# Attention with a gated FFN on one core: the loads of head 0 in order of need on one queue, its second block's query halves shifted by VectorE copies, later projections emitted sooner

## The chip, the cores and the metric

The kernel runs on one core of a Trainium2 chip. The metric is the device time of one execution in microseconds (us). A trace shows one run.

Names of engines: PE is TensorE (matmul), DVE VectorE, ACT ScalarE, POOL GpSimd, SP the engine that here only issues DMAs (the page lists no busy time for it). The granted clock is the share of TensorE's full pace that the trace records; "half clock" is 0.5. "L483" is a line of the kernel. The change shifts lines a little: L483 and L484 of before are L488 and L489 after it, L420 is L425, L425 is L430, L512 is L517.

## The reference

```python
xn = layernorm(x)                                   # x: 2048 x 640
q  = (xn @ wq) -> 32 heads of 192                   # k_cache, v_cache: 32 x 2048 x 192
s  = concat_heads(softmax(q k^T / sqrt(192)) v) @ wo
g  = silu((silu(x@w1) * (x@w3)) @ w2)               # the FFN gets xn too: 640 -> 1536 -> 640
out = x + s * g
```

Both parts get the normalised x. There are 32 heads, 4 blocks of 512 queries (`qb`), and 8 pairs of 128-key tiles (`p`) in a block. The work is one stream of (head, block, pair).

## The kernel before

Nearly all of it is TensorE: per pair six matmuls of scores (K times q), an exponential on ACT, and 16 matmuls of values. At `p == 0` of a block, TensorE also projects the queries of the *next* head for that block (`project`). Head 0 has no head before it, so its own projections (`project0`) stand inside its own stream, and everything they need is prepared while it runs: layer norm of x block by block on DVE, transposition of the normalised x (`xn`) into `xnT`, a copy of `xnT` with the two halves of the partitions swapped (`xnS`, by DMA), and for every q tile the pieces `qC` with its halves moved to the other partitions. K of later heads comes transposed by DMA (`load_k`); K of head 0 comes plain (`kn`) and is transposed by TensorE (`turn_k0`), copied by ACT, and one of its five windows is shifted to the other half of the partitions (`shift_k0`).

```python
    def load_k0():                                         # [cut]
        nc.scalar.dma_start(out=kn, in_=A_k_cache[0, 0].rearrange("(p t) d -> p (t d)", p=P))
    def shift_k0(j0):                                      # [cut]
        nc.vector.tensor_copy(out=KW[0:64, 3, ks], in_=KW[64:P, 0, ks])
    def move_q(qAB, qC, half):
        nc.gpsimd.dma_start(out=qC[0:64, half, :], in_=qAB[half][64:P, :])
        if half == 0:
            nc.gpsimd.dma_start(out=qC[64:P, 0, :], in_=qAB[0][0:64, :])
    def project0(qb):                                      # [cut: 10 matmuls from xnT]
        cast_pair(qAB, ps)                                 # qA by DVE, qB by ACT
        move_q(qAB, qC, 0)
        move_q(qAB, qC, 1)

    def head_start():
        load_x(0, 0, 2)                                    # SP's queue
        load_k0()                                          # ACT's queue
        load_x(0, 2, 4)
        load_w0()                                          # POOL's queue: weights of heads 0 and 1
        load_x(1)
        load_v(0)
        load_w(1)
        for g in range(2, NQB):
            load_x(g)
        turn_over(40)                                      # filler matmuls
        # [cut: layer norm of x block 0]
        turn_k0(pk0, 0, range(4)); copy_k0(pk0, 0); turn_over(6)
        ln_turn(0, 0, nc.vector.tensor_copy); turn_over(6) # transposes of xn
        # [cut: the other halves]
        swap_halves(0)                                     # xnS, SP's queue
        copy_k0(pk1, NPAIR // 2); project_first(); scores(0); shift_first()
        shift_k0(0); shift_k0(NPAIR // 2); scores(1)       # [cut]

    for n, (h, qb, p) in enumerate(stream):
        if p == 0 and n > 0: project(h + 1, qb)            # [cut]
        if h == 0 and qb == 0 and p == 3: project(1, 0)
        if h == 0 and qb + 1 < NQB and p == (6 if qb == 0 else 4):
            project0(qb + 1)
        scores(n + 2)                                      # two pairs ahead
        values(n)
        # [cut] for head 0: layer norm of block qb + 2 at p = 2 to 6, its transposes by DMA on SP's
        # queue; at p == 4 of block 0 the last x transposes of block 1;
        # at (qb == 1, p == 0) load_k(1), load_v(1) on SP's queue
```

All of this is in program order, and the order counts: in the change x's transposes stand behind kn's in TensorE's list and started at 11.09 us, after kn had come; put ahead of them (d_x_first below) they started at 8.14.

## Time and profile before

| | |
|---|---|
| time | 1954.48 us (3 runs, 1954.23 to 1954.80) |
| profiled span | 1952.9 us |
| PE busy | 1933.8 us, 99% |
| PE pauses in the first 75 us | 13.8 us in all |
| granted PE clock | 1.0 from its first record at 8.1 us on, but for 6.8 us after 35.4 us, when it was 0.5, and the end |

The page of the kernel before, the line of the engines' busy times and the first line of the chain that ended last:

```profile
PE 1933.8 (99%) x27281; PEld 1390.5 (71%) x27289; DVE 652.7 (33%) x990; ACT 1179.6 (60%) x1276; POOL 285.9 (15%) x511
...
PE 98%; DMA 1%; issue 0%; DVE 0%; POOL 0%; SPq 0%; DVEq 0%; POOLq 0%
```

So TensorE sets the time from end to end, and a change can only gain by taking pauses (or slow clock) out of TensorE's stream. These are the pauses of 1.5 us and more; all lie before 75 us. The columns are who waited, for whom, total us, how often, the longest (the three for qC are 3.04 us in block 1, 1.47 in block 2 and 0.45 in block 3):

```profile
PE st L484 <- DMA qC<-qA: 5.0, 3, 3.0
PE pk L564 <- POOL ident_bf masks.py:199: 2.8, 1, 2.8
PE st L483 <- DVE qA L425: 1.8, 1, 1.8
PE ps L420 <- DMA xnS<-xnT: 1.6, 1, 1.6
PE pst L352 <- DVE xn L344: 1.5, 1, 1.5
```

The largest lie together, at the first scores of block 1. TensorE's timeline there (start, duration, engine, line, operation, output<-inputs, and in brackets the idle time before it with what ended it):

```profile
34.78 0.39 PE L483 MATMUL st<-qA,KW 64*128 64x512 bf16 x1 [1.78 <-DVE qA L425]
38.21 0.58 PE L484 MATMUL st<-qC,KW 64*128 64x512 bf16 x1 [3.04 <-DMA qC<-qA]
```

TensorE projected block 1, needed the result at once, and stood until DVE had cast it and the DMAs had moved its halves. The second matmul took 0.58 in place of 0.38 us, at a granted clock of 0.50 (in each stretch of 1 us from 36 to 42 us). In the stretch from 35 to 40 us (last three columns: granted clock, DMA share, GB/s) it reads 0.54:

```profile
35.00:40.00 5.00, 1.96 (x12) 0.65 (x12) 0.74 (x2) 0.13 (x1) 1.59 (x3) 0.54 0.80 155
```

The loads of the start (last figure: median us from issue to landing):

```profile
kn<-in_A_k_cache_dram ACTq DMA_DIRECT2D x1, 768.0 KB, 5.4
vt<-in_A_v_cache_dram SPq DMA_DIRECT2D x1, 768.0 KB, 13.4
x_all<-in_A_x_dram SPq DMA_DIRECT2D x2, 320.0 KB, 5.8
W<-in_A_wq_dram POOLq DMA_DIRECT2D x2, 160.0 KB, 7.6
```

Last, what SP did for head 1 around that pause.

SP's timeline of issues, the load of K and V for head 1, then block 3's x transposes:

```profile
41.13 5.24 SPq L252 DMA_TRANSPOSE KW<-in_A_k_cache_dram  x1
46.42 2.89 SPq L253 DMA_TRANSPOSE KW<-in_A_k_cache_dram  x1
49.35 1.22 SPq L292 DMA_DIRECT2D vt<-in_A_v_cache_dram  x2
54.83 7.38 SPq L358 DMA_TRANSPOSE xnT<-xn  x4
```

### The profile page before, as it was taken

Reading aid. Unit: us, or ns where it says so; the run is one execution under the profiler, and the core shown is the slowest. Engines: PE = TensorE matmul, PEld = TensorE weight load, DVE = VectorE, ACT = ScalarE, POOL = GpSimd, SP = SyncE. Lnnn points to the kernel's source line nnn. Section 1 sums busy time; section 2 is a strip of 40 time slices with the busy share of each in tenths; the row PEclk is TensorE's granted clock in tenths of the full one; section 3 lists DMA queues with packets and bytes.
Section 4 is the critical chain, followed back from the end, with each engine's and each line's share of the span. In section 5 each row is a group of like instructions: output and inputs, shape, how many; then the busy total and the mean of one; then the engine's idle time right before and its main releaser. Section 6 shows DMA issues by size and latency. Waiting matters only on the chain.

```text
span 1952.9 us, 59687 instructions
## 1 busy us (share of the span) xinstructions
PE 1933.8 (99%) x27281; PEld 1390.5 (71%) x27289; DVE 652.7 (33%) x990; ACT 1179.6 (60%) x1276; POOL 285.9 (15%) x511
## 2 busy tenths in 40 slices
PE   7999999999999999999999999999999999999998
PEld 5677777777777777777777777777777777577776
DVE  6333333333333333333333333333333334521111
ACT  4667676767677767677777767776767677210000
POOL 3211111111111111111111111111111110000000
PEclk9999999999999999999999999999999999999999
DMA  8633242333343433353434332433323230837873
GB/s 189 126 61 89 56 96 60 96 68 94 64 100 68 100 68 100 67 157 68 100 67 101 68 98 67 100 68 75 88 58 96 58 82 2 242 77 139 155 151 60
DMA packets 394691, 179.57 MB, mean 92 GB/s; under 512 B 341648, under 2 KB 382864, under 8 KB 394432
## 3 DMA queue, kind: packets, MB, share of 16 engines
q1 hardware_dynamic: 372080, 125.98, 30.0%
q0 software_dynamic: 19760, 46.30, 9.9%
q8 instruction: 215, 3.52, 0.8%
q10 hardware_dynamic: 2592, 3.41, 0.6%
q14 instruction: 44, 0.36, 0.1%
HBM read 52.82 MB, written 27.79 MB: 41 GB/s over the span
## 4 chain that ended last, share of the span: by engine, by line
PE 98%; DMA 1%; issue 0%; DVE 0%; POOL 0%; SPq 0%; DVEq 0%; POOLq 0%
PE obank L512 35%; PE st L483 30%; PE ps L420 14%; PE ps_s L111 11%; PE st L484 3%; PE ps_f L718 3%; PE ps_gu L692 1%; DMA xnS<-xnT 0%; DMA qC<-qA 0%; DMA x_all<-in_A_x_dram 0%; PE ps L407 0%; DVE stats L316 0%; POOL qC L375 0%; DVE qA L425 0%; POOL rstd L325 0%
## 5 line engine op out<-in xcount | busy, mean ns | idle before, releaser
L486 ACT ACTIVATE pT<-st 128x1024 bf16<-128x1024 f32 x1024 | 1046.3, 1022 | 263.1 <-PE st L484 247.6
L512 PEld LDWEIGHTS <-pT 64*128 64x128 bf16 x16384 | 748.0, 94 | 209.0 <-issue 0.8
L512 PE MATMUL obank<-vt,pT 64*128 64x193 bf16 x16384 | 870.0, 244 | 0.0
L483 PE MATMUL st<-qC,KW 64*128 64x512 bf16 x2046 | 607.2, 377 | 0.3 <-DVE qC L393 0.3
L484 PE MATMUL st<-qC,KW 64*128 64x512 bf16 x1022 | 385.4, 377 | 5.0 <-DMA qC<-qA 5.0
L521 DVE COPY osum<-obank 128x772 f32<-128x772 f32 x128 | 123.1, 961 | 795.8 <-PE obank L512 795.8
L483 PE MATMUL st<-qA,KW 64*128 64x512 bf16 x1022 | 384.9, 377 | 2.0 <-DVE qA L425 1.8
L484 PE MATMUL st<-qB,KW 64*128 64x512 bf16 x1024 | 386.1, 377 | 0.0
L484 PE MATMUL st<-qA,KW 64*128 64x512 bf16 x1022 | 385.5, 377 | 0.0
L483 PEld LDWEIGHTS <-KW 64*128 64x128 bf16 x3068 | 278.2, 94 | 139.8 <-issue 7.9
L420 PE MATMUL ps<-xnT,W 64*128 64x512 bf16 x1280 | 299.4, 376 | 0.0
L420 PE MATMUL ps<-xnS,W 64*128 64x512 bf16 x1280 | 293.9, 377 | 1.6 <-DMA xnS<-xnT 1.6
L484 PEld LDWEIGHTS <-KW 64*128 64x128 bf16 x3068 | 279.0, 94 | 3.0 <-issue 2.1
L375 POOL DMA_DIRECT2D qC<-qA x127 | 66.7, 525 | 1298.4 <-DVE rl_all L528 1274.4
L420 PEld LDWEIGHTS <-W 64*128 64x128 bf16 x2560 | 141.7, 94 | 106.5 <-issue 1.9
L426 ACT CAST qB<-ps 128x512 bf16<-128x512 f32 x131 | 76.7, 585 | 230.1 <-PE ps L420 225.1
L111 PE MATMUL ps_s<-wo_sb,oT 128*128 128x384 bf16 (+3 forms) x1535 | 208.8, 300 | 0.1
L111 PEld LDWEIGHTS <-oT 128*128 128x128 bf16 x1536 | 148.1, 98 | 60.7
L522 DVE TENSOR_TENSOR osum<-osum,obank 128x772 f32<-128x772 f32 x128 | 122.7, 959 | 13.4
L529 DVE TENSOR_TENSOR ostage<-osum,rl_all 128x768 bf16<-128x768 f32 x128 | 122.6, 958 | 5.0 <-DMA o_scr<-ostage 0.7
L461 DVE SCALAR_TENSOR_TENSOR hT<-pt,qB 64x512 bf16<-64x512 bf16 x64 | 43.8, 684 | 199.1 <-ACT pt L460 199.1
L425 DVE CAST qA<-ps 128x512 bf16<-128x512 f32 x131 | 90.5, 691 | 29.5 <-PE ps L420 16.5
(79 smaller groups left out, 623.5 us busy)
## 6 DMA issues: line engine op xcount, KB each, us to landing
o_scr<-ostage SPq DMA_DIRECT2D x16, 1536.0 KB, 10.2
vt<-in_A_v_cache_dram SPq DMA_DIRECT2D x62, 384.0 KB, 5.5
qC<-qA POOLq DMA_DIRECT2D x254, 64.0 KB, 1.9
qC<-qB POOLq DMA_DIRECT2D x127, 64.0 KB, 2.3
wo_sb<-in_A_wo_dram POOLq DMA_DIRECT2D x1, 7680.0 KB, 36.3
W<-in_A_wq_dram POOLq DMA_DIRECT2D x32, 160.0 KB, 3.4
W<-in_B_w_dram POOLq DMA_DIRECT2D x32, 80.0 KB, 3.2
W<-in_A_wq_dram POOLq DMA_DIRECT2D x32, 80.0 KB, 2.9
```

What stands on the lines that cost most here:

```text
L111: nc.tensor.matmul(ps[:, 0:w], lhsT=oT[:, k, :], rhs=wo_sb[:, k, c0:c1], start=(k == 0), stop=(k == OC - 1))
L375: nc.gpsimd.dma_start(out=qC[0:64, half, :], in_=qAB[half][64:P, :])
L420: nc.tensor.matmul(ps[:, r * 512:(r + 1) * 512], lhsT=W[rows, j, :], rhs=xs[rows, j // 2, qs], start=(j == 0), stop=(j == 2 * DC - 1))
L425: a = nc.vector.tensor_copy(out=qAB[0][:], in_=ps[:, 0:512])
L426: b = nc.scalar.copy(out=qAB[1][:], in_=ps[:, 512:1024])
L483: nc.tensor.matmul(st2[:, 0:512], lhsT=ka, rhs=qa, start=r == 0 and nr == 3, stop=r == nr - 1)
L484: nc.tensor.matmul(st2[:, 512:1024], lhsT=kb, rhs=qb2, start=r == 0 and nr == 3, stop=r == nr - 1)
L486: nc.scalar.activation(out=pT2[:], in_=st2[:], func=ACT.Exp, scale=att_scale)
L512: nc.tensor.matmul(obanks[r][:, j * 256:j * 256 + DH + 1], lhsT=pT2[r * 64:(r + 1) * 64, t * 512 + j * P:t * 512 + (j + 1) * P], rhs=vt[r ...
L521: nc.vector.tensor_copy(out=osum[:], in_=ov[0])
L522: nc.vector.tensor_tensor(out=osum[:], in0=osum[:], in1=ov[1], op=ALU.add)
L529: nc.vector.tensor_tensor(out=ostage[:, qb * 4:qb * 4 + 4, hg * DH:(hg + 1) * DH], in0=osum[:, :, 0:DH], in1=rl.unsqueeze(2).to_broadcast( ...
```

## The change

Its intent: let x of block 0 come first and the rest of head 0's loads in the order in which they are needed, all on SP's queue; take the K shift off DVE; move block 1's query halves by DVE copies (0.29 us each) in place of DMAs; and emit the projections of blocks 1 to 3 one or two pairs sooner, so that casts and moves hide behind a pair.

```diff
 def load_k0():
-        nc.scalar.dma_start(out=kn, ...)
+        nc.sync.dma_start(out=kn, ...)
 def shift_k0(j0):
-        nc.vector.tensor_copy(out=KW[0:64, 3, ks], in_=KW[64:P, 0, ks])
+        nc.gpsimd.dma_start(out=KW[0:64, 3, ks], in_=KW[64:P, 0, ks])
 def project0(qb):
-        move_q(qAB, qC, 0)
-        move_q(qAB, qC, 1)
+        if qb == 1:
+            nc.vector.tensor_copy(out=qC[64:P, 0, :], in_=qAB[0][0:64, :])
+            nc.vector.tensor_copy(out=qC[0:64, 0, :], in_=qAB[0][64:P, :])
+            nc.vector.tensor_copy(out=qC[0:64, 1, :], in_=qAB[1][64:P, :])
+        else:
+            move_q(qAB, qC, 0)
+            move_q(qAB, qC, 1)
 def head_start():
         load_x(0, 0, 2)
+        load_x(0, 2, 4)
         load_k0()
-        load_x(0, 2, 4)
 [cut]
         load_w(1)
-        for g in range(2, NQB):
-            load_x(g)
 [cut]
         copy_k0(pk0, 0)
+        shift_k0(0)
 [cut]
         copy_k0(pk1, NPAIR // 2)
+        shift_k0(NPAIR // 2)
+        for g in range(2, NQB):
+            load_x(g)                       # now behind swap_halves(0) on SP's queue
         project_first()
         scores(0)
         shift_first()
-        shift_k0(0)
-        shift_k0(NPAIR // 2)
 main loop:
-        if h == 0 and qb + 1 < NQB and p == (6 if qb == 0 else 4):
+        if h == 0 and qb + 1 < NQB and p == (5 if qb == 0 else 2):
             project0(qb + 1)
```

More of the change, by code (lines that the diff above doesn't have):

```diff
@@ L261, in load_k0 @@
         kn = k0["kn"][:].rearrange("p t c -> p (t c)")[:, 0:NKT * DH]
-        nc.scalar.dma_start(out=kn, in_=A_k_cache[0, 0].rearrange("(p t) d -> p (t d)", p=P))
+        nc.sync.dma_start(out=kn, in_=A_k_cache[0, 0].rearrange("(p t) d -> p (t d)", p=P))
         k0["v"] = kn.rearrange("p (j c) -> p j c", c=2 * DH)
```

## The prediction

> **What bounds the kernel now.** TensorE: the page gives 1933.8 us busy of a 1952.9 us span (99%), and the chain of waits is 98% PE. All that can be won lies in the first 75 us; later the change touches nothing. TensorE's waits there (waits and timeline, 0 to 75 us): 2.75 us for the identity; 1.46 for the first normalised x (xn); 0.5+0.3+0.3 around the first scores; 1.56 for xnS, the swapped halves of xnT; 1.78 for the qA cast and 3.04 for the qC moves of block 1; 1.47 and 0.45 for the qC moves of blocks 2 and 3. The windows of 1 us show a granted clock of 0.50 from 36 to 42 us, so 38.21 to 42.86 holds work of 2.6 us at full pace: 2 us more. [...]
>
> **Costs and gains.**
> 1. kn moves from ACT's queue to behind x block 0 on SP's. Now the first x half lands at about 6.3 us, sharing 350 to 430 GB/s with kn. From cumulated bytes I estimate x half one at 4.3 us, kn at 7.1 (now 6.1). The warm-up ends at 7.0 anyhow, so kn's 16 transposes (1.58) and 6 fillers end near 9.1; there the x transposes start, not at 10.36. Gain 1.2 us (0.5 to 1.5).
> 2. x blocks 2 and 3 (1.3 MB) no longer precede the xnS swap, which took 9.6 us to land (later ones 3.6 to 5). The 1.56 us wait goes; about 0.2 remains for PSUM held by the qA cast. The K shift by DMA frees 0.5 us of DVE. Gain 1.4.
> 3. Block 1: project0 goes one pair earlier, and three DVE copies (0.29 each) replace DMAs of 1.9 to 2.8 us. The waits of 1.78 and 3.04 and the 2 us of clock go. New: project0 follows the transposes directly and waits about 0.9 us for DVE's xnT copy (0.82). Gain 6.
> 4. Blocks 2 and 3: project0 two pairs (2.6 us) earlier hides the moves: 1.47+0.45+0.2. But all is now 9 us earlier, and block 3's xnT transposes queue on SP behind the load of K for head 1 (issue 5.24+2.89 us). I expect project0 of block 3 to wait for xnT 0 to 2.6 us, and 0.3 us each for xnT of block 2 and for DVE freeing obank. Net 0.3.
>
> Sum: 1.2 + 1.4 + 6 + 0.3 = about 9 us, nearly all on the critical path, because TensorE hardly pauses afterwards. That is 0.5%.
>
> **Predicted time: 1945.5 us, 1942 to 1949 eight times in ten. Faster by over 2%: 0.01; within 2%: 0.98; slower: 0.01.**
>
> **What would show each step.** (1) First DVE statistics near 4.5 us, x transposes near 9. (2) No PE wait on xnS, landing in about 5 us. (3) No PE wait on qC in block 1, granted clock 1.0 from 30 to 45 us, a short wait on the xnT copy. (4) No wait on qC of blocks 2 and 3; possibly one on DMA xnT before block 3's projection. PE busy falls by about 2 us (clock); the time after 75 us is unchanged.
>
> **What would make it wrong.** kn landing after 8.5 us (gain 1 gone); the K shift, or V of head 0, late among the loads; x block 2 so late behind the swap that DVE holds the casts; the wait for block 3's xnT exceeding 3 us[...]. In the other direction, K's load issuing faster (3.0+2.4 us, as for head 2): 1944 or below.

1.2 + 1.4 + 6 + 0.3 is 8.9, its "about 9 us", and the 2 us of clock in the 6 is read from the trace of before (0.50 from 36 to 42 us).

## More of the kernel before

DVE's timeline, the norm of block 2's last two tiles:

```profile
34.94 0.80 DVE L344 TENSOR_SCALAR xn<-x_all,mv,rstd 128x640 bf16<-128x640 bf16 x2 [0.21 <-POOL rstd L325]
```

## The result

The changed kernel takes 1952.86 us (median of 4 runs, 1951.70 to 1953.43), the kernel before 1954.64 us (4 runs, 1954.23 to 1955.28). The ratio is 0.999, 95% interval 0.9973 to 1.0007. (A ratio here is the mean time of one kernel's fast runs over that of the other's of the same rounds, so not quite the ratio of the medians that are quoted.) Predicted was 1945.5 us, 1942 to 1949. It is the same within 2%, as predicted, but of the 9 us only 1.8 came, and the time lies outside the range.

The pauses of TensorE of 0.8 us and more in the first 75 us of the changed kernel, to be held against those of before:

```profile
PE ps L407 <- DMA xnT<-xn: 3.1, 1, 3.1
PE st L489 <- DMA qC<-qA: 3.0, 1, 3.0
PE pk L569 <- POOL ident_bf masks.py:199: 2.8, 1, 2.8
PE pk L272 <- DMA kn<-in_A_k_cache_dram: 2.6, 1, 2.6
PE st L488 <- DMA KW<-KW: 1.0, 1, 1.0
PE ps L407 <- DVE xnT L354: 0.9, 1, 0.9
PE obank L517 <- DVE osum L527: 0.8, 1, 0.8
```

The waits that the change aimed at are gone (qA, xnS, xn, and qC of block 1), and four others stand there, for kn, KW, xnT, and qC of block 2, which was 1.47 us before. All four are DMAs. Where they lie in TensorE's timeline:

```profile
9.85 1.07 PE L272 MATMUL pk<-ident_bf,kn 128*128 128x128 bf16 x16 [2.65 <-DMA kn<-in_A_k_cache_dram]
...
19.82 0.39 PE L488 MATMUL st<-qC,KW 64*128 64x512 bf16 x1 [0.97 <-DMA KW<-KW]
...
53.51 0.37 PE L489 MATMUL st<-qC,KW 64*128 64x512 bf16 x1 [2.97 <-DMA qC<-qA]
...
64.22 2.32 PE L407 MATMUL ps<-xnT,W 128*128 128x512 bf16 x9 [3.13 <-DMA xnT<-xn]
```

The loads of the start, now:

```profile
kn<-in_A_k_cache_dram SPq DMA_DIRECT2D x1, 768.0 KB, 8.1
vt<-in_A_v_cache_dram SPq DMA_DIRECT2D x1, 768.0 KB, 16.9
x_all<-in_A_x_dram SPq DMA_DIRECT2D x2, 320.0 KB, 3.2
...
W<-in_A_wq_dram POOLq DMA_DIRECT2D x2, 160.0 KB, 8.8
```

x of block 0 came 2.6 us sooner (3.2 against 5.8 us from issue), but kn took 8.1 where it had taken 5.4, V 16.9 where it had taken 13.4, and the weights 8.8 for 7.6. DVE's timeline of the changed kernel, block 2's last norms:

```profile
37.76 0.80 DVE L344 TENSOR_SCALAR xn<-x_all,mv,rstd 128x640 bf16<-128x640 bf16 x2 [0.81 <-POOL rstd L325]
```

SP's issues in the changed kernel, head 1's loads and block 3's transposes:

```profile
43.45 5.59 SPq L252 DMA_TRANSPOSE KW<-in_A_k_cache_dram  x1
49.08 4.28 SPq L253 DMA_TRANSPOSE KW<-in_A_k_cache_dram  x1
53.41 1.21 SPq L292 DMA_DIRECT2D vt<-in_A_v_cache_dram  x2
54.66 6.16 SPq L358 DMA_TRANSPOSE xnT<-xn  x4
```

The load of K for head 1 starts 2.3 us *later* than before, although TensorE is 6 us further: SP's list has block 2's x transposes in front of it, they wait for the norms, and DVE does the norms 2.8 us later. Between two norms DVE now waits 0.71 us for block 1's projection, does its cast and three copies (till 34.2 us), and then waits 0.85 us for ACT; before, it went straight on with the next work, and the cast came later.

### The ledger

The start of the same piece of work in both traces says where the time went. `best3` is the best kernel found, told below.

| TensorE starts, us | before | after | sooner by | best3 |
|---|---|---|---|---|
| first scores of head 0 | 15.66 | 16.30 | -0.64 | 14.66 |
| first projection of head 1 (in block 0) | 21.76 | 23.56 | -1.80 | 20.76 |
| scores that follow it | 25.66 | 25.72 | -0.06 | 22.92 |
| projection of head 1 in block 1 | 42.86 | 36.49 | +6.37 | 33.53 |
| the same in block 2 | 59.61 | 55.95 | +3.66 | 49.48 |
| the same in block 3 | 75.83 | 74.38 | +1.45 | 65.78 |
| end of the profiled span | 1952.9 | 1951.6 | +1.3 | 1942.8 |

Differences of neighbouring rows: the start lost 0.64, the K shift 1.16, the swap gained 1.74, block 1 gained 6.43, block 2 lost 2.71, block 3 lost 2.21. The sum is 1.45, and after 76 us nothing changes. Block 1 gave 6.43 of the 9 us that were promised. Of what had been gained at 36 us, 4.92 was given back within 40 us.

The first two rows are of one profile, and others share that start. d_kload_late, d_q2_dve, d_both and u_p4 (below) are the same program through block 0; in their traces the wait for kn (2.3 to 3.5 us) was followed by half clock (0.50 from 11 to 12 us in the first three; in u_p4 kn's 16 transposes took 1.86 us in place of 1.07), the first scores started at 17.20 to 18.79, and there was no wait for KW: from the first scores to head 1's first projection they took 6.10 us, as before the change. So the loss of 0.64 is the mildest of five, and the 1.16 of the K shift appears in this profile alone, where TensorE came to the shifted K soonest. By the first projection of head 1 all five had lost 1.5 to 3.1 us.

### The profile page after: what moved, and what is told of

Read it like the earlier page. It is cut to its first block, busy times and chain, and to the rows that moved or that the text cites. A ratio compares the mean times of both kernels' runs of the same rounds, so it can differ in the third digit from the quotient of the medians.

```text
span 1951.6 us, 59687 instructions
## 1 busy us (share of the span) xinstructions
PE 1930.7 (99%) x27281; PEld 1320.4 (68%) x27289; DVE 653.5 (33%) x991; ACT 1180.7 (60%) x1276; POOL 285.6 (15%) x510
## 4 chain that ended last, share of the span: by engine, by line
PE 97%; DMA 1%; issue 0%; DVE 0%; POOL 0%; SPq 0%; DVEq 0%; POOLq 0%
PE obank L517 35%; PE st L488 33%; PE ps L425 14%; PE ps_s L111 11%; PE ps_f L723 3%; PE ps_gu L697 1%; PE st L489 1%; DMA x_all<-in_A_x_dram 0%; DMA kn<-in_A_k_cache_dram 0%; DMA qC<-qA 0%; PE ps L407 0%; DMA xnT<-xn 0%; DVE qA L430 0%; PE pk L272 0%; POOL rstd L325 0%
## 5 line engine op out<-in xcount | busy, mean ns | idle before, releaser
L517 PEld LDWEIGHTS <-pT 64*128 64x128 bf16 x16384 | 715.0, 94 | 242.5 <-issue 1.3
L517 PE MATMUL obank<-vt,pT 64*128 64x193 bf16 x16384 | 853.1, 243 | 0.8 <-DVE osum L527 0.8
L425 PEld LDWEIGHTS <-W 64*128 64x128 bf16 x2560 | 123.4, 94 | 121.1 <-issue 0.2
L527 DVE TENSOR_TENSOR osum<-osum,obank 128x772 f32<-128x772 f32 x128 | 122.7, 959 | 13.4
```

Of the source, the lines that this page charges most:

```text
L425: nc.tensor.matmul(ps[:, r * 512:(r + 1) * 512], lhsT=W[rows, j, :], rhs=xs[rows, j // 2, qs], start=(j == 0), stop=(j == 2 * DC - 1))
L517: nc.tensor.matmul(obanks[r][:, j * 256:j * 256 + DH + 1], lhsT=pT2[r * 64:(r + 1) * 64, t * 512 + j * P:t * 512 + (j + 1) * P], rhs=vt[r ...
L527: nc.vector.tensor_tensor(out=osum[:], in0=osum[:], in1=ov[1], op=ALU.add)
```

## The experiments

17 kernels were run. All outputs are right. Names: `u_` is the change with a part undone, `d_` the change with one thing done differently, `b_` and `b1_` start from the kernel before and from `best1`. Medians are of 4 or 5 runs; the kernel before, beside them on the same chip, had medians between 1954.2 and 1955.2.

| kernel | median us | range | what it is |
|---|---|---|---|
| before | 1954.2 to 1955.2 | | |
| after | 1952.86 | 1951.70 to 1953.43 | the change |
| u_kn_act | 1951.25 | 1950.11 to 1954.92 | kn on ACT's queue |
| u_shift_dve | 1951.72 | 1949.08 to 1954.19 | K shift on DVE |
| u_p4 | 1954.31 | 1953.32 to 1956.09 | blocks 2, 3 projected at pair 4 |
| d_kload_late | 1951.77 | 1951.16 to 1953.61 | K, V of head 1 loaded a block later |
| d_q2_dve | 1952.89 | 1951.08 to 1954.71 | block 2's halves by DVE |
| d_both | 1948.34 | 1947.94 to 1949.79 | the load later, halves of 1 to 3 by DVE |
| b_block1 | 1951.37 | 1950.66 to 1953.50 | before, with block 1's part alone |
| d_x_first | 1954.98 | 1953.97 to 1957.72 | x transposes ahead of kn's |
| d_w1_late | 1955.30 | 1953.68 to 1957.57 | head 1's weights issued at 13 us |
| d_w1_mid | 1952.54 | 1951.66 to 1954.16 | the same at about 8.5 us |
| best1 | 1945.58 | 1945.49 to 1945.84 | all mended, kn on ACT's queue |
| b1_kn_sp | 1947.19 | 1943.82 to 1948.04 | best1, kn on SP's queue |
| b1_shift_dma | 1945.37 | 1945.13 to 1946.70 | best1, K shift by DMA |
| b1_w1_mid | 1945.52 | 1945.34 to 1945.74 | best1, weights later |
| best2 | 1947.75 | 1946.92 to 1948.51 | b1_kn_sp, weights later |
| best3 | 1944.49 | 1944.18 to 1944.54 | best1, block 0's x and kn on two queues |

### The two late waits: u_p4, d_kload_late, d_q2_dve, d_both

The theory: both late waits come from the one load of K for head 1. Its packets fill the DMA engines (DMA share 1.13 to 1.16 in the stretches of 5 us from 45 to 60 us), so that the 64 KB moves of q, issued at 45.98 us, take 6.4 us where others take 1.9; and its issue holds SP's queue from 43.45 to 54.6 us, and block 3's x transposes stand behind it. The rival: DVE or POOL are late, or the sooner projections were a mistake as such. The moves in the changed kernel:

```profile
qC<-qA POOLq DMA_DIRECT2D x2, 64.0 KB, 6.4
```

d_kload_late:

```diff
-        if qb == 1 and p == 0:
+        if qb == 2 and p == 0:
             load_k(1)
             load_v(1)
```

> The change with the loads of K and V for head 1 issued at the start of query block 2 of head 0 in place of block 1. Theory S (this load is what both late waits come from: its packets delay the qC moves of block 2, and its issue holds SP's queue before the xnT transposes of block 3): the wait of 2.97 us on qC and the wait of 3.13 us on xnT both go, qC moves land in 2 to 3 us, total 1946.5 to 1948. Rival (DVE or POOL come too late with qA or xn): both waits stay and the total stays at 1952.9.

Measured: both waits went, as the theory has it. The same moves, issued at 46.11 us (45.98 in the change) with the load out of the way, took

```profile
qC<-qA POOLq DMA_DIRECT2D x2, 64.0 KB, 1.9
```

A new wait came, for block 3's q moves, which now ran into the load at its new place (load issued from 59.97, moves at 62.41 to 63.43 us; TensorE waited for them till 69.54):

```profile
69.54 0.37 PE L489 MATMUL st<-qC,KW 64*128 64x512 bf16 x1 [2.57 <-DMA qC<-qA]
```

The total, 1951.77, missed the forecast of 1946.5 to 1948: I had put the load just before another set of moves. The wait follows the load, which is what the theory says.

d_q2_dve:

```diff
-        if qb == 1:
+        if qb in (1, 2):
             nc.vector.tensor_copy(out=qC[64:P, 0, :], ...)
```

> The change with block 2's query halves also shifted by DVE, K's load where it was. The wait of 2.97 us on qC goes. Theory S says the xnT transposes of block 3 are held by SP's queue, which this doesn't touch, so the wait on xnT before block 3's projection grows from 3.1 to about 5.5 to 6 us, and the total gains under 0.7 us[...]. Rival (block 3's xnT follows TensorE's and DVE's pace): the wait on xnT stays at 3 us and the total falls by 3 us, to 1950.

Measured: 1952.89 us, against 1952.86 of the change: nothing gained, though a wait of 2.97 us is gone. TensorE now comes to block 3's projection sooner and stands there:

```profile
62.35 3.17 PE L407 MATMUL ps<-xnT,W 128*128 128x512 bf16 x10 [3.56 <-DMA xnT<-xn]
```

The wait grew from 3.13 to 3.56, less than the 5.5 to 6 that I expected: the K load too went quicker with no moves beside it (SP through with it at 52.8 in place of 54.6 us). The ten matmuls took 3.17 us, where the change's nine took 2.32, and the granted clock over 60 to 80 us was 0.91 (1.00 in the change): a drop of the clock took the rest. So the two waits are in series: mending the first alone buys next to nothing.

d_both puts the two together, with `if qb >= 1:` for the copies:

> Both late waits taken away at once: K and V of head 1 loaded at query block 2, and the halves of blocks 2 and 3 shifted by DVE too. Each alone gave 1 us or nothing: with the load late the moves of block 3 ran into it (2.6 us on qC), with DVE copies the wait moved to xnT (3.6 us). Theory S: now neither is left, no TensorE wait over 1 us between 45 and 80 us, and the total falls by about 5.5 to 6 us below the change: 1946 to 1948. Rival: the waits have another source (DVE too full, or DMA crowded without K's load as well), and the total stays over 1950.

Measured: 1948.34 us, inside the forecast, 4.5 us under the change. Between 45 and 80 us TensorE waits once, for 0.8 us:

```profile
PE obank L517 <- DVE osum L527: 0.8, 1, 0.8
```

u_p4 undoes the last line of the change (pair 4 in place of 2):

> The change with the projections of blocks 2 and 3 back at pair 4. If going earlier by two pairs is what made the wait on xnT, and the qC wait of block 2 comes from K's load whatever the pair: wait on xnT 0.5 us or less, wait on qC of block 2 4 to 5.5 us (moves issued 2.6 us later, landing little later), total 1952 to 1954, no better than the change. Rival (p at 2 is simply the wrong choice): the total falls to 1950 or below.

Measured: 1954.31 us, just above the forecast. The wait on xnT was gone, and the waits on block 2's q pieces were 2.14 and 1.59 us, 3.7 together (4 to 5.5 expected), with slow matmuls after them (0.63 us each in place of 0.38, up to about 61 us). The place of the projection chooses which of the two waits is paid; it doesn't pay less.

### Block 1 alone: b_block1

The kernel before with the copies for `qb == 1` and with pair 5 in place of 6, nothing else:

> The kernel before with the block 1 part alone: its halves by DVE copies, its projection at pair 5; nothing else. Theory (block 1's pause was also the time in which K of head 1 was loaded; filling it brings TensorE to blocks 2 and 3 before that load is through): the first projection of query block 1 starts about 6 us earlier than before (42.86), then the qC wait of block 2 grows from 1.5 to 4 us or more and the total ends within 2.5 us of before: 1952 to 1954. Rival (the rest of the change ate the gain, not the load): total 1948 to 1949.

Measured: 1951.37 us, 3.8 us under the kernel before of the same rounds. That lies between the two forecasts. The trace: the projection of head 1 in block 1 starts at 35.90 (6.96 sooner than before), in block 2 at 55.09 (4.52 sooner), in block 3 at 72.25 (3.58 sooner). So the mechanism is the theory's, at about half the size that I gave it: 3.4 us of 7 are given back, 0.9 of it to a longer qC wait (2.41 in place of 1.47), 1.05 to a wait for xnT and 0.8 to one for DVE freeing obank; the rest is not accounted for. The theory's wording is not quite what the trace of before shows: head 1's K was not loaded during the pause in block 1 (33.0 to 38.2 us) but issued from 41.13 on. The pause held TensorE back, so that SP was through with the load (50.6) when block 2's moves were issued (53.74). The run also suggests that the rest of the change cost time: this part alone is 1.5 us faster than the whole by the medians, though the ranges overlap, and 2.1 us by the last row of the two ledgers (3.58 against 1.45), one profile each.

### The start: u_kn_act, d_x_first, u_shift_dve

u_kn_act is one word of the diff (`nc.sync` back to `nc.scalar` for kn):

> The change with one part undone: K of head 0 (kn) goes back to ACT's queue, still issued beside x block 0. Theory A (one queue alone moves less than two, so kn landed at 9.8 us where I reckoned 7.1 with the rate that two queues reached together): kn lands by 7.2 us, TensorE's wait of 2.65 us for kn goes to under 0.3, the x transposes start at 9.0 to 9.7 in place of 11.09, scores start near 14.7 (16.30 in the change). Total about 1.5 us faster than the change (1951.3). Rival B (the bytes ahead of kn and the W loads set it, whichever queue): kn lands no earlier than 9 us and the time stays at 1952.9.

Measured: kn was there by 7 us and its wait gone, as theory A has it. But x came late again, 6.1 us from issue, so the x transposes waited for it till 10.45, and no start gain was left: 1951.25 us, range 1950.11 to 1954.92, which overlaps that of the change, 1.6 under it by the medians. The profiled run was the slowest of the four. One reason stands in the stretches of 1 us: a pause of 1.92 us ending at 10.45 was followed by half clock (as was the wait for xnT of 3.25 us later: 0.50 from 66 to 68 us).

```profile
10.00:11.00 1.00, 0.55 (x8) 0.48 (x9) 0.75 (x3) 1.00 (x2) 0.87 (x2) 0.85 1.08 194
11.00:12.00 1.00, 1.00 (x12) 1.00 (x11) 0.99 (x3) 0.32 (x1) 0.57 (x1) 0.50 1.15 132
```

d_x_first leaves the loads as the change has them and turns TensorE's list round:

```diff
-        turn_k0(pk0, 0, range(4)); copy_k0(pk0, 0); shift_k0(0)
-        turn_over(6)
         ln_turn(0, 0, ...); turn_over(6)
-        turn_k0(pk1, NPAIR // 2, range(2))
         ln_turn(0, 1, ...)
-        turn_k0(pk1, NPAIR // 2, range(2, 4))
         swap_halves(0)
+        turn_k0(pk0, 0, range(4)); copy_k0(pk0, 0); shift_k0(0)
+        turn_k0(pk1, NPAIR // 2, range(4))
```

> The change with TensorE's program order of the start turned to the order in which data now arrives: both x transposes ahead of kn's. Theory: the change brought x to DVE 2.8 us earlier (3.48 against 6.32 us) and it bought nothing only because TensorE's program still has kn's transposes in front and kn came at 9.8. Then the x transposes start near 8.6 us, kn's about 10.3 without a wait for kn over 0.3 us, scores start near 15.5 (16.3 in the change); the total gains about 0.8 us, 1952.1, unless the DMA of the K shift (landing at 19.7 us) or the swap of xnS (landing at about 23 us) gives it back: they hang on the crowded queues, not on TensorE, so I expect under 0.5 us of it to reach the first projection of head 1.

Measured: the x transposes started at 8.14 and the wait for kn was gone, as expected; but TensorE then waited 1.46 us for the weights of head 0, and 3.98 us for the shifted K, which took 9.2 and 10.4 us to land. (The list of waits puts the 3.98 down to DVE, which had long been done; the weight load of the same matmul names the DMA of KW.) The total was 1954.98, slower than the change by 2.1. I had foreseen that the crowded queues would take the gain, not that they would take three times as much.

u_shift_dve puts the two K shifts back on DVE, at their old place:

> The change with the K shift of head 0 back on DVE, at its old place. The wait of 0.97 us for KW by DMA goes. If that wait is worth its length, the first projection of head 1 starts 1.15 us earlier and the total is 1951.7. Rival, which I believe: the xnS swap landed only about 23.0 to 23.7 us in the change, just as TensorE came to it, so the wait returns as a wait for xnS of 0.5 to 1.2 us and the total moves by under 0.6 us.

Measured: 1951.72, and from the first scores to the first projection of head 1 it took 6.10 us (18.87 to 24.97) in place of 7.26: 1.16 shorter. No wait for xnS came. But neither question is settled by it. The start of this profiled run was slow (kn's first transposes and the fillers after them took 2.33 us in place of 1.24), so TensorE came to the shifted K 2.6 us later than in the change; the four kernels named under the ledger came late too, and took the same 6.10 us with the shift by DMA. And TensorE came to the first xnS only at 24.99 us, where the swap had landed by 23.7 in the change, so the rival's late swap did not arise. The totals of the two kernels overlap.

### All mended: best1

```diff
 against the change:
+ kn on ACT's queue            (as u_kn_act)
+ K shift on DVE               (as u_shift_dve)
+ q halves of blocks 1 to 3 by DVE, head 1's K and V loaded at qb == 2   (as d_both)
-        if qb == 0 and p == 4:
+        if qb == 0 and p == 3:
             ln_turn(1, 1, nc.vector.tensor_copy)      # last x transposes of block 1
```

> The part of the change that worked (block 1, x blocks 2 and 3 behind the swap) with the rest mended: kn on ACT's queue, K shift on DVE, halves of blocks 1 to 3 on DVE, load of head 1 at query block 2, the last x transposes of block 1 one pair earlier (takes the 0.9 us wait on xnT's copy). Expect 1944 to 1946.5: the d_both figure less 0.9 for the transposes and about 1 for the start.

Measured: 1945.58 us, five runs within 0.35 us; ratio to before 0.9954 (0.9941 to 0.9968). This is what I had forecast for the change itself.

### What the kn queue and the K shift are worth when nothing hides it: b1_kn_sp, b1_shift_dma

> best1 with kn back on SP's queue, as the change has it: the price of the single queue with nothing behind it that hides it. kn lands at 9.5 to 10, wait on kn 2.3 to 3 us, V and the xnS swap later too. Theory A: 1.5 to 3 us slower than best1 (1945.6): 1947 to 1948.6. Rival: same within 0.5 us.

Measured: median 1947.19, 1.6 us slower than best1, with a wait of 2.7 us for kn in the profiled run. But the five runs fall in two groups: 1943.82 and 1944.16, and 1947.19 to 1948.04. So this kernel is usually 1.6 to 2.5 us slower than best1, and in two runs it was 1.4 to 1.8 us faster. That kn landed early in those two is likely but not shown: they have no profile.

> best1 with the K shift of head 0 by DMA, as the change has it. With kn on ACT's queue these DMAs took about 4 us to land in place of 7 (issued near 11 and 14.5). TensorE needs the first half at 17.9, the second at 20.5: no wait on KW, DVE free 0.5 us sooner; within 0.5 us of best1 (1945.1 to 1946.1). If the DMA shift is bad in itself, a wait on KW of about 1 us comes back and the total is 1946.5.

Measured: 1945.37, no wait on KW. The shift by DMA cost nothing here, with kn on ACT's queue: it took 4.7 us, and about 7 in the change. So the shift is not a fault in itself. That the single queue's crowd made it slow in the change is argued, not shown: with the same single queue it took 5.3 us in u_p4 and 6.2 in d_both (medians of two).

### Why kn is late: d_w1_late, d_w1_mid, b1_w1_mid, best2, best3

The rival for kn's lateness was the load of head 1's weights, which POOL issues between 4.4 and 6.6 us. d_w1_late issues them after the K shifts (about 13 us):

> The change with the weights of head 1 issued after the K shifts, out of the first 12 us. Rival B of the kn question (the weight loads' packets delay kn, not the single queue): kn lands by 8.3 us and TensorE's wait on kn falls from 2.65 to about 1. If it is the single queue: kn still lands at 9 to 10 us. The total I expect unchanged or worse by up to 1 us (weights of head 1 land near 20 to 22 us, when they are needed).

Measured: kn landed 5.7 us after issue, its wait was 0.8, the first scores started at 13.82. That spoke for the weights. (The total got worse, 1955.30: TensorE waited 2.6 us for those weights at the first projection of head 1.) d_w1_mid issues them after block 0's norms, about 8.5 us:

> The change with the weights of head 1 issued after block 0's second rstd on POOL (about 8.5 us) in place of 4.4 to 6.6. If those weights are what delays kn on the single queue: kn lands by 8 us, wait on kn under 1 us, scores start at 13.8 to 14.3 (16.3 in the change), weights land by 18 us and nobody waits for them. The total gains less than the 2 us of the start, because the K load of head 1 still stands in the way of blocks 2 and 3: 1950 to 1952.5. If not: kn at 9.5 or later and scores at 16 or later.

Measured: kn took 8.2 us again and TensorE waited 3.3 us for it. Up to 8.5 us this program is the same as d_w1_late, so the weights can't be what told the two apart. d_w1_late, unedited:

> d_w1_late without any edit, for a second sample of kn's landing. If its first look was a rare quick run: kn now takes 7.8 to 9 us from issue, wait on kn 2.3 us or more. If the weights of head 1 are the cause: 5.5 to 6 us again.

Measured (one run, of unknown state, 1958.29 us): kn 8.7 us from issue, wait 3.4. The same holds without anything downstream to hide it:

> b1_kn_sp with the weights of head 1 issued at that same later place: kn on the single queue and nothing downstream that eats the gain. If the weights were the cause: wait on kn under 1 us, scores start near 14, no clock drop at the start, total 1943 to 1944.5, about 1.5 us under best1 (1945.6). If the single queue costs by itself: 1946.5 to 1947.5 as b1_kn_sp.

> best1 (kn on ACT's queue, beside x) with the weights of head 1 issued later. x and kn still share the rate, so x's first half lands at 5.5 to 6 us (5.8 in best1) and scores start at 15 to 15.5: total 1945 to 1945.6. If the weights alone set the start whatever the queues, scores start near 14 and the total equals best2's.

Measured: best2 1947.75 (kn 7.9 us, wait 2.4), b1_w1_mid 1945.52, the same as best1. The weights are not it. Over all profiles, kn on SP's queue behind x took 7.5 to 9.0 us in eleven of twelve and 5.7 in one; on ACT's queue beside x it took 5.2 to 5.4 in six of six.

best3 asks whether it is the number of hardware queues (the pages list SP's as q1 and ACT's as q10, both `hardware_dynamic`, and POOL's as q0, `software_dynamic`). It keeps the order of need, and splits x of block 0 and kn over SP's and ACT's queue:

```diff
     def load_x(g, t0=0, t1=4):
-        nc.sync.dma_start(...)
+        (nc.scalar if t0 else nc.sync).dma_start(...)       # t0 > 0: second half of block 0
 def load_k0():
-        nc.scalar.dma_start(out=kn, in_=src)
+        nc.sync.dma_start(out=kn[:, 0:half], in_=src[:, 0:half])
+        nc.scalar.dma_start(out=kn[:, half:], in_=src[:, half:])
```

> best1 with block 0's x and kn each split over the two hardware queues, in order of need: x halves one on each, then kn's halves one on each. If it is the single queue that is slow with the weight loads beside it: first x half by 4.3 us, both kn halves by 7 us, no wait on kn over 0.3 us, x transposes near 9, scores near 14.2, total 1944 to 1944.6 (best1 1945.6). If kn's lateness has to do with x going first rather than with the queue: kn at 8 us or later, wait on kn 1 us or more, total 1945.5 to 1947.5.

Measured: 1944.49 us, five runs within 0.36 us, 1.1 us under best1; ratio to before 0.9946 (0.9933 to 0.996), 8.4 us under the change. Its loads of the start:

```profile
kn<-in_A_k_cache_dram ACTq DMA_DIRECT2D x1, 384.0 KB, 6.1
kn<-in_A_k_cache_dram SPq DMA_DIRECT2D x1, 384.0 KB, 6.5
x_all<-in_A_x_dram ACTq DMA_DIRECT2D x1, 320.0 KB, 4.1
x_all<-in_A_x_dram SPq DMA_DIRECT2D x1, 320.0 KB, 4.3
```

Its largest pauses of TensorE in the first 75 us:

```profile
PE pk L572 <- POOL ident_bf masks.py:199: 2.8, 1, 2.8
PE obank L520 <- DVE osum L530: 1.5, 2, 0.8
PE pk L275 <- DMA kn<-in_A_k_cache_dram: 0.5, 1, 0.5
```

x came 1.5 us sooner than before, and kn's transposes start at 7.73, 2.1 us sooner than in the change (the prediction's 7.1 was 0.6 too early even so); the first scores started at 14.66 (14.2 expected; kn's wait was 0.5, not under 0.3). The DMA rate says the same. From 4 to 6 us x and kn are in flight in all three kernels (last two columns: DMA share, GB/s). The kernel before:

```profile
4.00:6.00 2.00, 2.00 (x21) 2.00 (x20) 0.00 (x0) 0.00 (x0) 2.00 (x4) 1.00 0.98 376
```

The change:

```profile
4.00:6.00 2.00, 2.00 (x22) 2.00 (x20) 1.90 (x7) 1.11 (x3) 2.00 (x4) 1.00 0.78 236
```

best3:

```profile
4.00:6.00 2.00, 2.00 (x22) 2.00 (x20) 0.90 (x3) 1.09 (x3) 2.00 (x4) 1.00 1.01 379
```

With x and kn on one hardware queue the DMA engines were busy 78% of that stretch and moved 236 GB/s (all queues together, so with the weights); with two they were full and moved 376 to 379. The change is at the low end: in the nine slow single-queue profiles in which this stretch was read it has 236 to 333 GB/s, in the quick one 389, and in the five with two queues 370 to 380 (in the other four, reckoned from finer slices of the first 9 us, about 237 and 307 with one queue, 369 and 379 with two). Why the DMA engines moved less with one queue, and why one profile in twelve is quick, stays open: no run here shows it.

## Why the prediction was wrong, point by point

The right parts first. TensorE as the bound and 75 us as the only stretch that matters: right, nothing changed after 76 us. Step 2, the swap: 1.4 predicted, 1.74 measured, but partly by luck: the swap was to land in about 5 us and took 8.1, so that its second half was there at about 23.7 us, just as TensorE came to it, 1.8 us later than before. best1 (its swaps land in 3.5 to 6.5 us, no wait, TensorE there at 21.62) shows that the step holds when the start is not late. Step 3, block 1: "Gain 6" predicted, 6.43 measured, with the new wait of 0.9 us for xnT's copy where it was expected (0.92) and the granted clock at 1.00 from 30 to 45 us. The size of the class (within 2%) was right.

**The step that failed most is step 4, "Net 0.3"; it measured -4.9** (2.71 lost in block 2, 2.21 in block 3). I had seen that everything would be 9 us earlier and that block 3's transposes queue behind the load of K for head 1, and I allowed 0 to 2.6 us for it; it was 3.13 (over 3 us was named under what would make it wrong). What I did not see is that the q moves of block 2, which the change gave two pairs more time, would be issued *into* that load. I costed them at the 1.9 to 2.8 us that they take elsewhere and they took 6.4, so the slack of 2.6 us was not enough and TensorE waited 2.97 us. In the kernel before they were issued at 53.74, when SP had finished issuing the load at 50.6. d_kload_late and d_both show that it is this load: the waits follow it, and without either collision they are gone. I also took the load's start to move forward with TensorE. It moved back, from 41.13 to 43.45, because block 1's cast and copies, which step 3 praises, and DVE's waits around them now stand in front of block 2's norms. b_block1 shows that this give-back belongs to block 1's gain itself: 3.4 of 7 us were lost again with nothing else changed.

**Step 1, "Gain 1.2 us (0.5 to 1.5)", measured -0.64** (-1.5 to -3.1 in the four other profiles with this start). The failing term is "kn at 7.1": it landed at 9.8. I worked it out from cumulated bytes with the rate of the kernel before, 350 to 430 GB/s, which two hardware queues had reached together. With x and kn on one queue the change moved 236 GB/s from 4 to 6 us. The prediction named this under what would make it wrong ("kn landing after 8.5 us"), and gave it no weight in the range. x did land when expected or sooner (DVE started at 3.48, 4.5 predicted). best3 shows that the idea of the step was right and its means wrong: order of need on two queues gained 1.0 us at the first scores.

**"The K shift by DMA frees 0.5 us of DVE", in step 2**, measured -1.16 in this profile: the first shift was issued at 12.27 because kn was late, took about 7 us, and TensorE waited 0.97 us for it. It is not a loss of every run: the four kernels with the same start show none. b1_shift_dma shows that the shift is harmless with kn on time.

As a sum: predicted 1.2 + 1.4 + 6 + 0.3, measured -0.64 + (1.74 - 1.16) + 6.43 - 4.92 = 1.45.

What stays open is the scatter of the runs. After a pause the clock dropped in some traces and not in others. It dropped in the kernel before around block 1's pauses of 1.78 and 3.04 us (0.50 from 36 to 42 us), in u_kn_act after 1.92 us (0.50 from 11 to 14) and after 3.25 (0.50 from 66 to 68), and after waits for kn of 2.39 us in best2 and 2.74 in b1_kn_sp (0.50 from 12 to 14 in both). It did not after 2.14 us at the same place in b1_w1_mid (1.00 from 8 to 12), nor after the change's 2.65, 2.97 and 3.13 us (1.00 up to 80 us). So the length of one pause does not decide it, and what does is not shown here. In u_kn_act each drop came to about 3.4 us at half clock (summed over its stretches of 1 us), so a pause costs a further 1.7 us (my estimate: half of that) or nothing, by whether the clock drops in that run. I take this, with kn's rare quick landings, for most of the 2 to 5 us of range that many kernels with such pauses show; the runs without a profile don't tell. best1, best3 and b1_w1_mid, which after the wait for the identity pause for at most 1.01, 0.8 and 2.14 us, repeat within 0.4 us.

## What to carry to other kernels

When a pause is taken out of an engine's stream, ask what it gave time to: a load that had been through before the next transfers were issued (here by 3 us) will meet them, and they were costed when they were alone (64 KB between partitions: 1.9 us alone, 6.4 to 6.7 beside the load of K; K shifts of the same size 3.1 to 10.4 us at the start). A wait taken out is a gain only as far as the next resource in line is early; look up how early it is (here two late waits in series: mended together 4.5 us, by either half of the cure nothing or 1). And a transfer rate read from a trace is that of the queues that made it (here 376 GB/s with two and 236 with one, from 4 to 6 us): when an edit merges two queues into one, the rate has to be measured again.
